# Value loads, the state update's bank and the second input product in the opening of a gated attention and feed-forward kernel

## The chip, the cores and the metric

The kernel runs on one core of a Trainium2 chip. The metric is the device time of one execution in microseconds (us). A second view is the profile of one execution, whose span runs from its first to its last instruction; all places in time ("at 63.95") are us from the start of that span.

## The reference

Two parts follow each other. The first is a gated linear attention: for each of 4 batches and 8 heads a state of 48 x 48 is carried over 768 tokens. The second is a feed-forward network over all 3072 tokens (4 x 768), with 384 inputs (8 heads x 48), 2048 hidden units and a leaky maximum.

```python
for t in range(S):
    state = alpha[:, :, t, :, None] * state + np.einsum('bhd,bhe->bhde', k[:, :, t], v[:, :, t])
    y[:, :, t] = np.einsum('bhd,bhde->bhe', q[:, :, t], state)
...
h = x @ w_in
g = np.maximum(0.01 * h, h)
return (g @ w_out).astype(np.float32)
```

q, k, v and alpha are float32. The two weights come as float64 and are read as pairs of 32-bit words.

## The kernel before, in words

**Units.** The attention is cut into 24 units: 6 blocks of 128 tokens, and in each block the 4 batches. Unit u is block u // 4 of batch u % 4. In a unit, the products of alpha along its 128 tokens turn the recurrence into matrix products: scores of keys against queries with a causal mask, times the values, plus the queries against the state that the earlier block of the same batch left. The first 9 units (0 to 8, AHEAD = 9) are done at the start, before the feed-forward part begins; units 9 to 23 are done later, mixed into it. Units 0 to 3 have no earlier state.

One of the first units goes through these functions:

- `load` (line 132) and `load_values` (156) issue transfers of alpha, q, k and v from SyncE's queue (SP). There are two buffers each for alpha, q and k and three for v, so a load of unit u + 2 (or u + 3 for v) takes the place of one that was used. From unit 9 on, the loads asked for early are put on a list and issued at the end of the weight loads.
- `turn_ahead` (295) transposes one of alpha, q, k on TensorE (PE) into a bank of PSUM, with `keep_warm` matmuls behind the first four, and then asks for the load that takes the buffer's place.
- `scans` (300) makes the running products on VectorE (DVE), and calls `next_state` for an earlier unit between its two scans.
- `scaled_q` (332), `scaled_k` (342), `scores` (352), `mask_scores` (361): scale, multiply on PE, copy to `sm` on ScalarE (ACT), mask on GpSimd (POOL). `mask_scores` then empties two lists on POOL: `scalings` (the new state, a product with the decay) and `parts` (see below).
- `outputs` (387) makes two PSUM banks of results y: the earlier state's part, then the masked scores times the values; then, in columns 256 to 447 of the first bank, the sum of keys times values `kv` for the state. For each of the two banks ACT makes a rounded copy in the high half of `large` (`xh`) and an exact copy `whole`; the difference, the low half, goes on the list `parts` for POOL (from unit 9 on DVE makes it at once).
- `next_state` (435) adds `kv` to the state on DVE (for units 0 to 3 ACT copies it), into `us`, and puts the scaling on the list.
- `gather` (449) moves, for three units, some rows of `large` to their places by two transfers. Gather 0, 1 and 2 belong to units 0 to 2, 3 to 5 and 6 to 8; each must wait until POOL has made the low halves of its units.

Where two engines read the same PSUM bank, the framework makes the second in the program's order wait for the first.

**Feed-forward.** The 16 blocks of 128 hidden units are the weight blocks. `load_weights` (199) fetches a block by four transfers of w_in and one of w_out into one of four buffers `raw`; `converting` (213) turns it into a high and a low float32 part in eight steps: ACT scales `raw`, DVE makes `bits` (two steps), `raw` and `pw`, ACT rounds the high half, DVE makes `raw` and the low half of `w`. Each step is put by hand between other work. An item is one weight block for the 384 tokens of three units. `ffn_in` (491) makes its input product (9 matmuls into `ph`), then ACT, DVE, ACT and DVE make `t`, `t`, `gh` and `gl`; conversion steps can be handed in to stand between these. `ffn_out` (518) makes its output product (9 matmuls), summed over all blocks in three PSUM banks, of tag b for the first three units and tag a for the next three. The first 32 items alternate between units 0 to 2 and units 3 to 5, block by block, while the blocks are converted. Output products follow their input products by two items, and by three from the ninth item on.

**What sets the order.** A helper at line 35 issues every operation behind the one before it on the same engine (so nearly all rows of the profile have line L35), until the third group of items begins. So in the opening each engine runs its instructions in the order in which they are written. The order of the opening is in lines 556 to 612: first loads, unit 0's start, a loop over units 0 to 7, then unit 8 (`last`), the conversion of block 1, and the first two items. In the loop, `WEIGHTS` says after which unit's scaling a weight block is asked for: block 1 at unit 5, block 2 at unit 6, block 3 at unit 7, each ahead of that unit's `outputs`; a gather stands behind the outputs. After the opening comes the main loop over items, whose first step asks for block 4; its transfers stand behind gather 2 in SP's queue.

Of the kernel before, what the change touches and what calls it, by code (L numbers as in the profile page):

```python
# [23 lines left out]
def gated_linear_attn_ffn(ctx, tc, q, k, v, alpha, w_in, w_out, out):  # L24
# [15 lines left out]
    B, H, S, D = q.shape  # L40
# [3 lines left out]
    C = 128  # L44
    NC = S // C
    NP = H // 2
# [4 lines left out]
    BR = HB + D  # L51
# [21 lines left out]
    AHEAD = 3 * UPB  # L73
# [8 lines left out]
    def bank(tag=None):  # L82
        if tag is None:
            tag = kinds[0]
            kinds.append(kinds.pop(0))
        return ps_x.tile([P, 512], F32, name=tag)
# [17 lines left out]
    state, vals_sb, rest = rest[:B], rest[B:B + NV], rest[B + NV:]  # L104
# [6 lines left out]
    def w_in_of(f, n, g):  # L111
        return w_sb[f][:, n, g * P:(g + 1) * P]
# [43 lines left out]
    def load_values(u):  # L156
        if u >= NU:
            return
        if u >= AHEAD and later is not None:
            later.append((load_values, u))  # L160
            return
        tb, b = units[u]
        made["v", u] = nc.sync.dma_start(
            vals_sb[u % NV].rearrange("t (h d) -> t h d", h=H),
            v[b, :, tb * C:(tb + 1) * C, :].rearrange("h t d -> t h d"),
        )
# [32 lines left out]
    def load_weights(f, part=None):  # L199

        if part != 1:
            jobs[f] = cvp.tile([P, 2 * NG, 2 * P], I32, name="raw", bufs=NRAW)
        raw = jobs[f]
        dst = raw.bitcast(I64) if f64 else raw[:, :, 0:P].bitcast(F32)
        for r, n, src, step, group in runs if part != 0 else ():
            a = w_in[src:src + n, f * P:(f + 1) * P]
            nc.sync.dma_start(
                dst[r:r + n, 0:NG], bass.AP(a.tensor, a.offset, [[step * DF, n], [group * DF, NG], list(a.ap[1])])
            )
        if part != 1:  # L210
            made["raw", f] = nc.sync.dma_start(dst[:, NG:], w_out[f * P:(f + 1) * P, :].rearrange("p (g f) -> p g f", g=NG))
# [71 lines left out]


    STEP = 16
    WEIGHTS = {5: 1, 6: 2, 7: 3}
    WARM = 16, 4, 3, 12
    warm = []

# [5 lines left out]
    def turn_ahead(u, i, name, **kw):  # L295
        turned[u, i] = transposed(u, i, name, **kw)
        if u < AHEAD:
            load(u + NL[i], i)
# [26 lines left out]
    def sum_up(u, which=(0, 1)):  # L325

        with behind("sm", u) if u >= AHEAD else nullcontext():
            for n in which:
                t = sums[u][n]
                nc.scalar.activation(t, t, AF.Abs, accum_out=acc[:, 2 * u + n:2 * u + n + 1])  # L330
# [11 lines left out]
    def scaled_k(u):  # L342
        pc, rc, pe, qs = live[u]
        turn_ahead(u, 2, "ks")
        kT = turned.pop((u, 2))
        if u >= AHEAD:
            load(u + NL[2], 2)
        ks = kT if u >= AHEAD else atp.tile([P, NP, C], F32, name="ks")
        made["ks", u] = nc.vector.tensor_tensor(ks, kT, rc, ALU.mult)
        live[u] = [pe, qs, ks]  # L350
# [36 lines left out]
    def outputs(u):  # L387
        tb, b = units[u]
        i, j = divmod(u, UPB)
        pe, qs, ktok = live[u][:3]  # L390
        V, W = vals_sb[u % NV], state[b]
        at = i % 3 * (NG + 1)
        banks = [bank(), bank()]
        y = [t.rearrange("r (p n) -> r p n", p=NP)[:, 0:2, :] for t in banks]

        def product(p, s, c, lhsT, rhs, **kw):

            nc.tensor.matmul(y[s][HB * c:HB * c + lhsT.shape[-1], p % 2, :], lhsT, rhs, skip_group_check=True, **kw)

        for n in range(2):  # L400
            for c in (0, 1):
                for s in (0, 1) if tb else ():
                    p, lo = 2 * c + n, HB * s
                    m = D if c else HB
                    product(p, s, c, W[lo:lo + D, p * D:p * D + m], qs[lo:lo + D, p, :], start=n == 0, stop=False)
        for n in range(2):
            for s in (0, 1):
                for c in (0, 1):
                    p = 2 * c + n
                    at_v, m = (2 * p + s) * D, D if c else HB  # L410
                    product(p, s, c, V[:, at_v:at_v + m], masked[u][s][:, p, :], start=not tb and n == 0, stop=n == 1)
        del masked[u]
        kv = None
        if tb < NC - 1:
            kv = banks[0][0:BR, 2 * C:2 * C + NP * D]
            for p in range(NP):
                for s, lo, m in ((0, 0, HB), (1, HB, D)):
                    h = 2 * p + s
                    made["kv", u] = nc.tensor.matmul(
                        kv[lo:lo + m, p * D:(p + 1) * D], ktok[:, p, lo:lo + m], V[:, h * D:(h + 1) * D],  # L420
                        start=True, stop=True, skip_group_check=True,
                    )
        load_values(u + NV)
        live[u] = pe, kv
        for s in (0, 1):
            xh, xl = (x_sb[0:BR, at + s:at + s + NG:2, n, j * C:(j + 1) * C] for n in (0, 1))
            nc.scalar.copy(xh, y[s][0:BR])
            if u < AHEAD:
                whole = atp.tile([P, 2, C], F32, name="whole")[0:BR]
                nc.scalar.copy(whole, y[s][0:BR])  # L430
                parts.append((xl, whole, xh.bitcast(F32), ALU.subtract))
            else:
                nc.vector.tensor_tensor(xl, y[s][0:BR], xh.bitcast(F32), ALU.subtract)

    def next_state(u):
        tb, b = units[u]
        pe, kv = live.pop(u)
        if kv is None:
            return
        W = state[b][0:BR]  # L440
        us = atp.tile([P, NP * D], F32, name="us")[0:BR]
        if tb == 0:
            nc.scalar.copy(us, kv)
        else:
            nc.vector.tensor_tensor(us, W, kv, ALU.add)
        W, us = (t.rearrange("d (p e) -> d p e", p=NP) for t in (W, us))
        scalings.append((W, us, pe[0:BR].broadcast_to([BR, NP, D]), ALU.mult))

    def gather(i):

# [40 lines left out]
    def ffn_in(i, f, steps=None):  # L491

        first, second = steps or ((), ())
        xh, xl = xs[i]
        ph = ps_h.tile([P, 512], F32, name="ph")[:, 0:TB]
        n = 0
        for g in range(NG):
            for wn, xt in ((HIGH, xh), (HIGH, xl), (LOW, xh)):
                nc.tensor.matmul(ph, w_in_of(f, wn, g), xt[:, g, :], start=n == 0, stop=n == 3 * NG - 1)
                n += 1  # L500
        t = ffp.tile([P, TB], F32, name="t")
        nc.scalar.mul(t, ph, 0.01)
        for step in first:
            next(step, None)
        nc.vector.tensor_tensor(t, ph, t, ALU.max)
        gh = ffp.tile([P, TB], F32R, name="gh", bufs=LAG + 1)
        nc.scalar.copy(gh, t)
        for step in second[:1]:
            next(step, None)
        gl = ffp.tile([P, TB], F32R, name="gl", bufs=LAG + 1)  # L510
        made["gl", i, f] = nc.vector.tensor_tensor(gl, t, gh.bitcast(F32), ALU.subtract)
        for step in second[1:]:
            next(step, None)
        return gh, gl
# [29 lines left out]
    items = []  # L544
# [3 lines left out]
    gs = {}  # L548
# [3 lines left out]
    def steps(conversion, n):  # L552
        for _ in range(n):
            next(conversion, None)
# [3 lines left out]
    load(0, 1)  # L558
    load(0, 2)
    load(1, 0)  # L560
    load_values(0)
    load(1, 1)
    load(1, 2)
    load_values(1)
    load_values(2)
    conversions = [converting(f) for f in range(EARLY + 2)]
    warm += WARM
    turn_ahead(0, 0, "e")
# [1 line left out]
    steps(conversions[0], 8)  # L570
    scaled_q(0)
    scaled_k(0)
    turn_ahead(1, 0, "e")
    for u in range(AHEAD - 1):
        scores(u)
        scans(u + 1, [u - 1] if u else [])
        mask_scores(u)
        k_tokens(u)
        scaled_q(u + 1)
        scaled_k(u + 1)  # L580
        if u + 2 < AHEAD:
            turn_ahead(u + 2, 0, "e")
        if u < AHEAD - 2:
            sum_up(u)
        else:
            steps(conversions[1], 1)
        if u in WEIGHTS:
            load_weights(WEIGHTS[u])
        outputs(u)
        if u % UPB == 0 and u:  # L590
            gather(u // UPB - 1)
            ready.add(u // UPB - 1)
    loaded_f = 1 + len(WEIGHTS)
    last = AHEAD - 1
    scores(last)
    mask_scores(last)
# [4 lines left out]
    gs[0] = ffn_in(*items[0][:2])  # L601
    new, coming = conversions[EARLY:]
    steps(new, 1)
    outputs(last)
    next_state(last)
    gs[1] = ffn_in(*items[1][:2], ((new, new), (new, new)))
    for todo in (scalings, parts):
        while todo:
            nc.gpsimd.tensor_tensor(*todo.pop(0))
# [5 lines left out]
    for n in range(len(items) + LAG):  # L615
# [3 lines left out]
        if n < len(items):  # L619
# [20 lines left out]
            elif i == 1:  # L640
                gs[n] = ffn_in(i, f, ((), (coming, coming, coming, coming)))
                new, coming = coming, converting(f + EARLY + 1)
# [148 lines left out]
```

## Time and profile before

| | us |
|---|---|
| median of 3 runs | 530.34 |
| lowest, highest | 529.16, 530.98 |
| profiled execution | 530.13 |
| its span | 528.4 |
| PE busy | 516.9 (98%) |
| DVE busy | 366.1 (69%) |
| ACT busy | 239.3 (45%) |
| POOL busy | 61.4 (12%) |

In rows of the timeline the columns are start, duration (from the first to the end of the last instruction merged in the row), engine, line, operation, tile written <- tiles read, sizes, and the count; in brackets the idle time of the engine before it and what ended that. SPq is the time in which SyncE issues a transfer, not the transfer itself. Tiles that stand in one allocation have one name: `small` holds the loads, the values and the states, `large` the inputs of the feed-forward part; a, b and ph are PSUM tags.

Rows of busy time by stretches have the length, then the busy time and count for each engine, the clock granted to PE (1.00 is full), the mean busy share of the DMA engines (transfers that overlap count twice, so it can pass 1) and GB/s.

### The profile page before, as it was taken

What the parts mean: (1) busy time and instruction counts of PE and PEld (TensorE: products, weight loads), DVE (VectorE), ACT (ScalarE), POOL (GpSimd) and SP (SyncE); (2) the same over time, 40 slices, a digit from 0 to 9 for tenths busy, and PEclk for the clock granted to TensorE, in tenths of its full rate; (3) what the DMA queues carried; (4) which work ended last, traced back from release to release, by engine and by line L of the source; (5) the groups of instructions that cost most, each with busy time, mean ns of one, the idle gap of its engine ahead of it and who ended that gap; (6) DMA issues with size and microseconds to landing.
All of it is one profiled execution on the core that took longest, in us unless ns stands there. A gap on an engine that the chain in (4) does not pass through costs nothing.

```text
span 528.4 us, 10355 instructions
## 1 busy us (share of the span) xinstructions
PE 516.9 (98%) x3986; PEld 495.0 (94%) x3986; DVE 366.1 (69%) x685; ACT 239.3 (45%) x533; POOL 61.4 (12%) x133
## 2 busy tenths in 40 slices
PE   8899899999999999999999999999999999999996
PEld 8788798999999899999999999999999999999996
DVE  6897799999969996787586585675787434333331
ACT  2597666656532544344334434345343444234332
POOL 2375810000000111000000000000000000000000
PEclk9999999999999999999999999999999999999999
DMA  9999885444905634442342422423301010101001
GB/s 155 166 162 158 188 176 167 130 133 140 203 3 143 174 91 98 94 102 70 71 107 42 115 69 58 93 56 87 70 1 39 1 46 2 24 0 47 0 1 50
DMA packets 92984, 46.65 MB, mean 88 GB/s; under 512 B 57857, under 2 KB 90113, under 8 KB 92929
## 3 DMA queue, kind: packets, MB, share of 16 engines
q1 hardware_dynamic: 92928, 45.93, 39.7%
q8 instruction: 33, 0.54, 0.4%
q14 instruction: 23, 0.18, 0.1%
HBM read 38.83 MB, written 4.72 MB: 82 GB/s over the span
## 4 chain that ended last, share of the span: by engine, by line
PE 85%; DVE 5%; DMA 4%; SPq 2%; ACT 1%; issue 1%; POOL 1%; DVEq 0%; ACTq 0%; POOLq 0%
PE ph L35 35%; PE b L35 34%; PE a L35 16%; SPq L35 2%; DMA small<-in_q_dram 1%; DMA small<-in_alpha_dram 1%; DVE t L35 1%; DVE gl L35 1%; DMA raw<-in_moe_w_out_dram 1%; POOL sm L35 1%; DVE bits L35 1%; DMA raw<-in_moe_w_in_dram 1%; DVE raw L35 1%; DVE pc L35 0%; ACT gh L35 0%
## 5 line engine op out<-in xcount | busy, mean ns | idle before, releaser
L35 PE MATMUL ph<-large,w 128*128 128x384 f32 x1152 | 223.4, 338 | 1.5 <-DVE w L35 1.0
L35 PEld LDWEIGHTS ph<-large,w 128*128 128x128 f32 x1152 | 200.6, 188 | 3.5 <-DVE w L35 1.4
L35 PE MATMUL b<-w,gh 128*128 128x384 f32 x672 | 173.8, 340 | 0.0
L35 DVE TENSOR_TENSOR t<-ph,t 128x384 f32<-128x384 f32 x128 | 70.4, 550 | 83.7 <-ACT t L35 83.7
L35 ACT ACTIVATE t<-ph 128x384 f32<-128x384 f32 x128 | 62.9, 492 | 139.5 <-PE ph L35 137.5
L35 PEld LDWEIGHTS b<-w,gh 128*128 128x128 f32 x672 | 119.9, 188 | 2.0 <-issue 0.5
L35 ACT CAST gh<-t 128x384 fp32r<-128x384 f32 x128 | 65.7, 514 | 106.4 <-DVE t L35 106.4
L35 PE MATMUL b<-w,gl 128*128 128x384 f32 x336 | 112.2, 335 | 0.0
L35 DVE TENSOR_TENSOR gl<-t,gh 128x384 fp32r<-128x384 f32 x128 | 70.9, 554 | 37.5 <-ACT gh L35 36.0
L35 PEld LDWEIGHTS b<-w,gl 128*128 128x128 f32 x336 | 63.0, 188 | 0.0
L35 POOL TENSOR_SCALAR_AFFINE_SELECT sm<-sm 128x512 f32<-128x512 f32 x33 | 23.5, 726 | 112.7 <-ACT sm L35 112.4
L35 PE MATMUL a<-qs,ks 48*128 48x128 f32 x312 | 29.8, 285 | 0.0
L35 PEld LDWEIGHTS a<-qs,ks 48*128 48x128 f32 x312 | 25.1, 187 | 4.3 <-issue 3.5
L35 DVE STREAM_TRANSPOSE ks<-small 128x512 f32<-128x512 f32 x15 | 16.7, 1123 | 14.6 <-PE a L35 14.0
L35 PE MATMUL a<-sm,small 128*48 128x128 f32 (+1 forms) x312 | 23.8, 279 | 0.9 <-POOL sm L35 0.9
L35 PE MATMUL a<-w,gh 128*128 128x384 f32 x96 | 24.6, 335 | 0.0
L35 POOL COPY pe<-pc 128x4 f32<-128x4 f32 x24 | 4.8, 200 | 165.9 <-DVE pc L35 165.9
L35 PEld LDWEIGHTS a<-sm,small 128*48 128x48 f32 (+1 forms) x312 | 16.9, 129 | 4.8 <-issue 3.1
L35 PE MATMUL ph<-small 128*128 128x128 f32 x120 | 16.9, 296 | 3.6 <-DMA small<-in_alpha_dram 2.0
L35 DVE TENSOR_TENSOR_SCAN pc<-e,small 128x128 f32<-128x128 f32 x60 | 20.0, 395 | 0.0
L35 DVE TENSOR_TENSOR_SCAN rc<-e,small 128x511 f32<-128x511 f32 x15 | 19.1, 1270 | 0.3
L35 POOL TENSOR_TENSOR small<-us,pe 112x192 f32<-112x192 f32 x20 | 10.5, 524 | 75.7 <-DVE us L35 69.3
(84 smaller groups left out, 545.2 us busy)
## 6 DMA issues: line engine op xcount, KB each, us to landing
raw<-in_moe_w_out_dram SPq DMA_DIRECT2D x16, 384.0 KB, 3.8
raw<-in_moe_w_in_dram SPq DMA_DIRECT2D x32, 144.0 KB, 3.2
small<-in_v_dram SPq DMA_DIRECT2D x24, 192.0 KB, 3.8
out_dram<-bits SPq DMA_DIRECT2D x18, 192.0 KB, 1.9
small<-in_alpha_dram SPq DMA_DIRECT2D x32, 96.0 KB, 2.3
small<-in_q_dram SPq DMA_DIRECT2D x30, 96.0 KB, 2.3
small<-in_k_dram SPq DMA_DIRECT2D x30, 96.0 KB, 2.2
small<-in_alpha_dram SPq DMA_DIRECT2D x30, 80.0 KB, 2.5
```

What stands on the lines that cost most here:

```text
L35: self.last = getattr(self.engine, op)(*args, **kw)
```

## The change

- The first three value loads are issued later: v0 behind unit 1's q and k, v1 behind unit 0's scaling (so behind unit 2's alpha, q and k), v2 in unit 0's pass behind unit 3's q and k.
- `kv` goes to the second y bank in place of the first. ACT's copies become a generator in two halves: the first bank's copies stay in `outputs`, and for units 0 to 7 the second bank's copies are made at the end of `next_state`, behind the sum that reads `kv`. Unit 8 makes both in `outputs`.
- Block 1 is still asked for at unit 5. Blocks 2 and 3 are asked for behind the outputs of units 6 and 7, so that block 2 comes behind gather 1.
- The second item's `ffn_in`, with four conversion steps of block 2 in it, stands ahead of unit 8's `outputs` and `next_state`.

```diff
-    WEIGHTS = {5: 1, 6: 2, 7: 3}
...
-            kv = banks[0][0:BR, 2 * C:2 * C + NP * D]
+            kv = banks[1][0:BR, 2 * C:2 * C + NP * D]
...
         load_values(u + NV)
         live[u] = pe, kv
+        rest = copies(u, at, j, y)
+        next(rest)
+        if u < AHEAD - 1:
+            halves[u] = rest
+        else:
+            next(rest, None)
+
+    def copies(u, at, j, y):
         for s in (0, 1):
             xh, xl = (x_sb[0:BR, at + s:at + s + NG:2, n, j * C:(j + 1) * C] for n in (0, 1))
             nc.scalar.copy(xh, y[s][0:BR])
...
                 nc.vector.tensor_tensor(xl, y[s][0:BR], xh.bitcast(F32), ALU.subtract)
+            yield
+
+    halves = {}
 
     def next_state(u):
...
         scalings.append((W, us, pe[0:BR].broadcast_to([BR, NP, D]), ALU.mult))
+        if u in halves:
+            next(halves.pop(u), None)
...
     load(1, 0)
-    load_values(0)
     load(1, 1)
     load(1, 2)
-    load_values(1)
-    load_values(2)
+    load_values(0)
...
     scaled_q(0)
     scaled_k(0)
+    load_values(1)
     turn_ahead(1, 0, "e")
...
         scaled_k(u + 1)
+        if not u:
+            load_values(2)
...
-        if u in WEIGHTS:
-            load_weights(WEIGHTS[u])
+        if u == AHEAD - 4:
+            load_weights(1)
         outputs(u)
         if u % UPB == 0 and u:
             gather(u // UPB - 1)
             ready.add(u // UPB - 1)
-    loaded_f = 1 + len(WEIGHTS)
+        if u > AHEAD - 4:
+            load_weights(u - AHEAD + 5)
+    loaded_f = 4
...
     steps(new, 1)
+    gs[1] = ffn_in(*items[1][:2], ((new, new), (new, new)))
     outputs(last)
     next_state(last)
-    gs[1] = ffn_in(*items[1][:2], ((new, new), (new, new)))
```

## The prediction before the result was known

> **What bounds the kernel now.** I read the page first, then busy time by stretches, then PE's row of the timeline from its idle times backwards.
>
> ```profile
> span 528.4 us, 10355 instructions
> PE 516.9 (98%) x3986; PEld 495.0 (94%) x3986; DVE 366.1 (69%) x685; ACT 239.3 (45%) x533; POOL 61.4 (12%) x133
> ```
> ```profile
> core 0: us, PE busy (x) PEld busy (x) DVE busy (x) ACT busy (x) POOL busy (x), PEclk, DMA share, GB/s
> 20.00:48.00 28.00, 27.98 (x413) 24.64 (x412) 24.32 (x55) 22.64 (x67) 18.05 (x39) 1.00 1.15 162
> 48.00:63.00 15.00, 12.62 (x205) 10.84 (x205) 11.57 (x22) 9.53 (x24) 10.63 (x15) 1.00 0.98 197
> 63.00:92.00 29.00, 27.96 (x165) 27.59 (x161) 27.41 (x45) 18.78 (x38) 4.23 (x5) 1.00 0.65 164
> 92.00:528.40 436.40, 431.83 (x3081) 416.26 (x3079) 288.83 (x534) 182.41 (x396) 23.66 (x56) 1.00 0.29 72
> ```
> From 92 us on PE is busy 431.83 of 436.40 us, so whatever comes early or late at 92 us comes so at the end. The change acts before that, and there are three limits in turn: transfers (DMA share 1.15) up to 48 us, the start of the feed-forward part, and DVE (27.41 of 29 us) from 63 to 92. PE's own rows show where each one ends last:
>
> ```profile
> 19.40 0.63 PE L35 MATMUL ph<-small 128*128 128x128 f32 x4 [1.68 <-DMA small<-in_alpha_dram]
> ...
> 48.38 0.66 PE L35 MATMUL ph<-small 128*128 128x128 f32 x4 [0.36 <-DMA small<-in_alpha_dram]
> ...
> 57.04 1.83 PE L35 MATMUL ph<-large,w 128*128 128x384 f32 x9
> ...
> 60.60 0.43 PE L35 MATMUL b<-sm,small 128*64 128x128 f32 x4 [1.15 <-POOL sm L35]
> 61.90 0.43 PE L35 MATMUL a<-sm,small 128*64 128x128 f32 x4 [0.87 <-POOL sm L35]
> ...
> 66.38 0.52 PE L35 MATMUL b<-w,gh 128*128 128x384 f32 x2
> ...
> 89.83 1.48 PE L35 MATMUL ph<-large,w 128*128 128x384 f32 x7 [1.04 <-DVE w L35]
> ```
> The last wait decides: at 89.83 PE has stood 1.04 us for the low half of weight block 5. So the end is set by the DVE chain that makes it, and PE time saved before 89.83 only lengthens this wait. Followed back, the DVE chain begins where ACT gets weight block 1 (55.40, a transfer):
>
> ```profile
> 55.40 0.92 ACT L35 ACTIVATE raw<-raw 128x768 f32<-128x768 f32 x1 [1.66 <-DMA raw<-in_moe_w_out_dram]
> ...
> 62.27 0.95 ACT L35 ACTIVATE raw<-raw 128x768 f32<-128x768 f32 x1
> 63.27 0.37 ACT L35 CAST large<-b 112x256 fp32r<-112x256 f32 x1
> ...
> 75.61 0.93 ACT L35 ACTIVATE raw<-raw 128x768 f32<-128x768 f32 x1
> 76.42 0.49 ACT L35 ACTIVATE t<-ph 128x384 f32<-128x384 f32 x1
> ```
> ```profile
> 62.40 0.57 DVE L35 TENSOR_TENSOR gl<-t,gh 128x384 fp32r<-128x384 f32 x1 [0.58 <-ACT gh L35]
> 63.95 0.35 DVE L35 TENSOR_TENSOR us<-small,b 112x192 f32<-112x192 f32 x1 [0.99 <-ACT whole L35]
> 64.23 0.56 DVE L35 TENSOR_SCALAR bits<-raw 128x768 int32<-128x768 int32 x1
> 64.83 1.14 DVE L35 SCALAR_TENSOR_TENSOR bits<-raw,bits 128x768 int32<-128x768 int32 x1
> ...
> 67.93 0.55 DVE L35 TENSOR_SCALAR pw<-bits 128x768 int32<-128x768 int32 x1
> 68.40 0.55 DVE L35 TENSOR_TENSOR t<-ph,t 128x384 f32<-128x384 f32 x1
> ...
> 77.27 0.55 DVE L35 TENSOR_TENSOR t<-ph,t 128x384 f32<-128x384 f32 x1
> ...
> 88.83 0.95 DVE L35 SCALAR_TENSOR_TENSOR w<-raw,pw 128x768 fp32r<-128x768 f32 x1
> ```
> After 63.95 no DVE row of this stretch carries a wait of note: what delays one of its steps delays block 5.
>
> **Value loads moved back.** Alpha of unit 2 now stands behind both v1 and v2:
>
> ```profile
> 11.37 2.18 SPq L35 DMA_DIRECT2D small<-in_v_dram  x2
> 13.66 2.32 SPq L35 DMA_DIRECT2D small<-in_alpha_dram  x1
> ```
> It moves up by those two issues, about 2.2 us, more than PE's wait of 1.68 at 19.40: that wait goes. The values cost nothing: v0, v1, v2 stay in SP's queue ahead of the alpha of units 2, 3, 4, whose transposes stand in PE's queue ahead of the outputs that read them. What is late next is alpha of unit 8. From alpha of unit 4 on the queue is as before, with the same bytes ahead; the transfers run without a pause (share 1.15, 162 GB/s), and PE already waits 0.36 us at 48.38. An earlier PE waits there for 0.36 + 1.68 = 2.04 us instead. Weight block 1, which ACT waits 1.66 us for at 55.40, is behind the same bytes too. I take nothing for this edit; its other end is -1.68 us (a rival below).
>
> **State update in the second bank, second copies behind it.** No instruction is added. For units 4 to 7 DVE's us step no longer waits for ACT's copies of the bank that holds the sum; ACT's second pair of copies waits for us instead. Units 4 to 6 lie before 48.38 or just around it, where PE waits for the transfer anyway: nothing. At the end, unit 7's second pair goes behind unit 8's score copies, so POOL's masking may start up to 0.7 us sooner (two ACT copies of 0.37, as at 63.27). That only shortens the PE waits at 60.60 and 61.90. Unit 8 itself does both pairs first, so its us keeps its wait for ACT.
>
> **Second input product ahead of unit 8's outputs.** On PE nine matmuls, at most 1.83 us as at 57.04, fill the waits of 1.15 and 0.87 us at 60.60 and 61.90. Its input, gather 1, is issued ahead of weight block 2, so about where that block starts now:
>
> ```profile
> 53.06 2.43 SPq L35 DMA_DIRECT2D raw<-in_moe_w_in_dram  x4
> ...
> 56.23 1.22 SPq L35 DMA_DIRECT2D large<-large  x2
> ```
> It comes 3.17 us sooner; block 2 comes later by the gather's 1.22 us of issue. PE gains up to 1.83 us, but loses it at the next step: the first output product (66.38) needs three banks of tag b, one of them unit 8's first y bank. ACT's copies free it, and ACT now does block 2's scaling, t and gh of the second product ahead of these copies. DVE's steps (bits twice, t, below) end about 2.1 us after 63.25, gh takes some 0.5 as t does on ACT (0.49 at 76.42), the two copies at most 0.74: the bank is free at about 66.5. PE stands where it stood at 66.38: nothing. If the bank were free at once, PE would be earlier and would wait longer for DVE at 89.83; nothing too.
>
> On DVE the 0.99 us wait at 63.95 goes, because block 2's conversion no longer stands behind us. ACT has scaled block 2 at 62.27 + 0.95 = 63.22 if the block lands in time, so bits starts at 63.25 instead of 64.23. With us (0.28 to the next row) behind, the chain gains about 0.7 us.
>
> **What the move does to POOL and SP.** us of unit 8 now stands behind bits, t, raw, gl and pw. In the rows these take from 64.23 to 68.40, 4.17 us, some 0.7 of which comes from sharing with POOL (bits 1.14 where others take 0.95, and a longer gl). So us starts at 63.25 + 3.5 to 4.2 = 66.75 to 67.4 and is done at 67.1 to 67.7, where now it is done at 64.3. POOL's last list waits for it:
>
> ```profile
> 54.55 1.42 POOL L35 TENSOR_TENSOR large<-whole,large 112x256 fp32r<-112x256 f32 x2
> 58.01 3.83 POOL L35 TENSOR_SCALAR_AFFINE_SELECT sm<-sm 128x512 f32<-128x512 f32 x2 [2.04 <-ACT sm L35]
> 61.82 1.74 POOL L35 TENSOR_TENSOR large<-whole,large 112x256 fp32r<-112x256 f32 x2
> 63.52 0.51 POOL L35 TENSOR_TENSOR small<-us,pe 112x192 f32<-112x192 f32 x1
> 64.39 0.77 POOL L35 TENSOR_TENSOR small<-us,pe 112x192 f32<-112x192 f32 x1 [0.36 <-DVE us L35]
> 65.12 2.47 POOL L35 TENSOR_TENSOR large<-whole,large 112x256 fp32r<-112x256 f32 x2
> ```
> Now: state of 8 at 64.39, two subtractions, done at 67.59. After the change three subtractions follow the state, since unit 7's second one is listed only after unit 8's masking. One costs 0.71 us alone (54.55), 0.87 at 61.82, 1.24 beside a busy DVE (65.12). POOL's end: at least 67.1 + 0.51 + 3 x 0.71 = 69.75, at most 67.7 + 0.77 + 3 x 1.24 = 72.2. DVE is as busy there as at 65.12, but its t steps and the us read one operand from PSUM, so I take 1.05 each: 67.3 + 0.6 + 3.15 = 71.0.
>
> The SBUF page of the Trainium skill (SBUF — State Buffer, Who interferes with whom) states that a DVE instruction with two SBUF inputs and a GpSimd one that reads SBUF exclude each other, and that the second to issue is blocked until the first is done. The trace agrees in kind (3.83 us for two selects at 58.01 beside DVE's conversion, 2.47 against 1.42 us for the subtractions); by that rule alone the sum would go to the upper end, 72.2.
>
> Behind POOL's end stand, in SP's queue, gather 2 and then weight block 4:
>
> ```profile
> 67.62 1.21 SPq L35 DMA_DIRECT2D large<-large  x2
> ...
> 71.34 0.58 SPq L35 DMA_DIRECT2D raw<-in_moe_w_out_dram  x1
> ```
> ```profile
> raw<-in_moe_w_out_dram SPq DMA_DIRECT2D x1, 384.0 KB, 3.9
> ```
> The last row is the answer on transfers for that one issue: 3.9 us to landing. So block 4 lands 71.34 - 67.62 + 3.9 = 7.6 us after POOL's end, now at 75.2. ACT scales it at 75.61: 0.4 us in hand. Behind the scaling in ACT's order stands t (76.42, done at 76.91), which DVE takes at 77.27: another 0.36. Nothing else can run in that place, since ACT and DVE take their steps in the written order. Together 0.7 to 0.8 us are in hand, and POOL's end moves by 71.0 - 67.6 = 3.4. DVE's t at 77.27 is then late by 3.4 - 0.7 = **2.7 us** (bounds: 69.75 gives 1.4, 72.2 gives 3.9). The 0.7 us that DVE gained before is swallowed in the wait. From 77.27 to 89.78 DVE has no gap to win it back in; PE, which waits for DVE at 89.83, starts as much later, and after 92 us it is full to the end.
>
> **The sum.** 0 (loads) + 0 (bank) + 0 (PE's product) + 2.7 (block 4): the profiled execution took 530.13 us (528.4 of span and 1.7 around it), 0.2 below the median of 530.34. So 530.13 + 2.7 = 532.8, likeliest 531.5 to 534.0.
>
> **Rivals.** (1) Block 4 is not late: POOL ends before about 68.3. For it: nothing but how rough spans on POOL are. Against: us alone comes 2.8 us later. Then only DVE's 0.7 us counts: 529.4. (2) The transfers do move up with PE, because SP's queue is held by PE's reading of the buffers and not by the transfers: the 1.68 us reach weight block 1 at 55.40 and all that follows. For it: many SP issues take 1 us or more and PE reads buffers just before. Against: share 1.15, and the wait at 48.38 falls on a transfer. With block 4 late all the same: 530.13 + 2.7 - 1.68 = 531.2. (3) Both, the faster side: 530.13 - 1.68 - 0.7 = 527.8; it needs alpha of unit 8 landing by 46.7 and POOL's end not over 0.7 us behind the shifted DVE. (4) The change does not fill PE's wait, since gather 1 lands too late for the second product: PE then waits at the product instead, and the chain over block 4 is as in the forecast, so its time is too.
>
> **Chances.** Forecast with (4): 0.62; (1) 0.13; (2) 0.15; (3) 0.08; 0.02 for anything else. A measurement here tells about 0.3%, 1.6 us, from no change. Slower by more: nearly all of the forecast, 0.60. Within: (1), (2), the forecast's low edge, 0.31. Faster: 0.09. The range reaches down to (1), 529.4, and up to 534.0.
>
> **What would show it.** Right: no alpha wait near 18 us and one of about 2 us before unit 8's transposes at 48.4; nine more ph matmuls ahead of the sm waits, which shrink; bits at 63.3; DVE's last us on the small state near 67; POOL's last large at 70 to 72; gather 2 right behind it; an ACT wait of 2 to 4 us on raw from w_out near 78; PE's wait for w at 89.8 grown to about 3 us in all. Wrong: unit 8's alpha or weight block 1 more than 1 us earlier; gather 2 issued before 68.3; no ACT wait on block 4; or PE resuming block 5 before 90 us.

## The result and the profile after

The kernel after takes 535.25 us (median of 5 runs, 534.96 to 537.24), the kernel before 530.41 beside it (529.16 to 531.06): a ratio of 1.0104, 95% interval 1.0078 to 1.0130. It is slower: the two medians differ by 4.84 us, and the ratio makes 5.5 us of 530.41. The profiled execution took 535.13 us, with a span of 533.4.

The first two lines of the page of after show PE's busy time up by 3.7 us and the span by 5.0:

```profile
span 533.4 us, 10346 instructions
PE 520.6 (98%) x3986; PEld 497.0 (93%) x3986; DVE 368.6 (69%) x685; ACT 240.3 (45%) x533; POOL 60.3 (11%) x133
```
Busy time by the stretches of the prediction, kernel after:

```profile
48.00:63.00 15.00, 15.00 (x219) 13.20 (x219) 11.44 (x20) 8.35 (x20) 8.34 (x13) 1.00 0.97 204
63.00:92.00 29.00, 24.43 (x124) 22.40 (x123) 24.61 (x40) 15.74 (x33) 4.40 (x4) 0.94 0.56 146
92.00:528.40 436.40, 435.67 (x3099) 419.92 (x3098) 292.95 (x540) 184.07 (x401) 23.57 (x56) 1.00 0.28 71
```
PE is now busy in the whole of 48 to 63, where it had stood 2.38 us, and loses more than that from 63 to 92: 24.43 of 29 us, where it had 27.96. DVE falls there from 27.41 to 24.61. That the engine which bounds this stretch has idle time again says that something ahead of it is late.

Four rows of the timeline of after, one each of POOL, SP's queue, ACT and DVE, are the chain of the prediction in order:

```profile
67.70 0.51 POOL L35 TENSOR_TENSOR small<-us,pe 112x192 f32<-112x192 f32 x1 [6.85 <-DVE us L35]
68.16 3.93 POOL L35 TENSOR_TENSOR large<-whole,large 112x256 fp32r<-112x256 f32 x3
```
```profile
72.12 1.21 SPq L35 DMA_DIRECT2D large<-large  x2
73.44 2.37 SPq L35 DMA_DIRECT2D raw<-in_moe_w_in_dram  x4
75.86 0.58 SPq L35 DMA_DIRECT2D raw<-in_moe_w_out_dram  x1
```
```profile
79.87 0.90 ACT L35 ACTIVATE raw<-raw 128x768 f32<-128x768 f32 x1 [3.69 <-DMA raw<-in_moe_w_out_dram]
```
```profile
81.18 0.56 DVE L35 TENSOR_TENSOR t<-ph,t 128x384 f32<-128x384 f32 x1 [3.34 <-ACT t L35]
```
POOL waits 6.85 us for us of unit 8 and ends at 72.09 (before: 67.59). Gather 2 stands right behind it (72.12), weight block 4 behind that (75.86, before 71.34), ACT waits 3.69 us for block 4, and DVE's t of the sixth item starts at 81.18, 3.91 us later than before. PE's rows with a wait, from 63 us on:

```profile
65.65 0.62 PE L35 MATMUL b<-w,gh 128*128 128x384 f32 x2 [0.62 <-DVE t L35]
66.74 1.83 PE L35 MATMUL ph<-large,w 128*128 128x384 f32 x9 [0.30 <-ACT whole L35]
71.56 1.48 PE L35 MATMUL ph<-large,w 128*128 128x384 f32 x7 [1.08 <-DVE w L35]
81.79 1.83 PE L35 MATMUL ph<-large,w 128*128 128x384 f32 x9 [0.81 <-DVE t L35]
...
87.54 2.31 PE L35 MATMUL ph<-large,w 128*128 128x384 f32 x7 [1.52 <-DVE w L35]
100.62 1.50 PE L35 MATMUL ph<-large,w 128*128 128x384 f32 x7 [0.29 <-DVE w L35]
```
With the 0.23 us at 85.43, which is left out here, these waits sum to 4.85 us, more than the nine matmuls that PE won at 57; before, only the 1.04 us at 89.83 stood here. Compared product by product, the input products start 4.5 to 4.6 us later than before from 102 to 168 us, 5.3 later from 192 to 426 and 5.0 later at the end.

**The zero of a single profile.** ACT starts to scale weight block 1 at 55.40 in the profile of before and at 54.72 in that of after. In the profiles of the experiments below it starts between 54.51 and 56.27; with the old order of the loads alone the four profiles have 54.79, 54.97, 55.40 and 56.27. These are single executions of different kernels, but before and delay_block4 differ in nothing ahead of this row, and they are 0.61 us apart. The nine profiles with the new loads have 54.51 to 55.09, so a part of the 0.68 us may also be a gain of the loads; one execution each can't tell. The end varies as well: from the t of the last item to the end of the span seven profiles take 9.6 to 9.8 us and six take 11.2 to 12.5, so only the spans of before and after, with 9.8 us each, are set side by side here. All later times of the opening are therefore counted from ACT's start on block 1: block 4's w_out issue and DVE's t of the sixth item, each minus ACT's start on block 1 in the same profile. For before these are 71.34 - 55.40 = 15.94 and 77.27 - 55.40 = 21.87; the table has the difference to these.

| kernel | ratio (95%) | ACT starts block 1 | block 4 issued later by | DVE's t later by |
|---|---|---|---|---|
| after | 1.0104 (1.0078-1.0130) | 54.72 | 5.20 | 4.59 |
| loads_alone | 0.9993 (0.9975-1.0011) | 54.68 | 0.01 | 0.01 |
| bank_alone | 1.0030 (1.0016-1.0044) | 54.97 | 2.28 | 1.82 |
| product_alone | 1.0053 (1.0034-1.0071) | 56.27 | 3.04 | 2.40 |
| after_without_bank | 1.0031 (1.0015-1.0046) | 54.52 | 3.02 | 2.39 |
| product_back | 1.0040 (1.0024-1.0056) | 54.77 | 2.35 | 2.53 |
| drain_early | 1.0061 (1.0043-1.0080) | 54.51 | 3.95 | 3.33 |
| delay_block4 | 1.0049 (1.0029-1.0069) | 54.79 | 2.60 | 1.75 |
| block4_first | 1.0016 (1.0000-1.0032) | 55.09 | early | 1.14 |
| no_bank_block4_first | 0.9993 (0.9977-1.0010) | 54.85 | early | 0.77 |
| drain_block4_first | 1.0012 (0.9995-1.0029) | 55.06 | early | 1.12 |
| dve_waits_filled | 0.9996 (0.9981-1.0012) | 54.70 | early | 0.35 |

In after, product_alone, after_without_bank and drain_early, where ACT waits 1.85 to 3.69 us for block 4, DVE's t is late by block 4's delay less 0.61 to 0.64 us. In delay_block4 it is less 0.85; there ACT has the block 3.78 us behind its issue (77.11 - 73.33), in these four 3.97 to 4.01. In bank_alone and product_back block 4 is later too, but t is not late because of it: ACT starts on the block 0.15 and 0.08 us behind its step before. Where these two lose is said below.

### The profile page after: what moved, and what is told of

It is laid out like the page before. It is cut to its first block, busy times and chain, and to the rows that moved or that the text cites. A ratio compares the mean times of both kernels' runs of the same rounds, so it can differ in the third digit from the quotient of the medians.

```text
span 533.4 us, 10346 instructions
## 1 busy us (share of the span) xinstructions
PE 520.6 (98%) x3986; PEld 497.0 (93%) x3986; DVE 368.6 (69%) x685; ACT 240.3 (45%) x533; POOL 60.3 (11%) x133
## 3 DMA queue, kind: packets, MB, share of 16 engines
HBM read 38.83 MB, written 4.72 MB: 82 GB/s over the span
## 4 chain that ended last, share of the span: by engine, by line
PE 78%; DVE 3%; ACT 1%; issue 0%; DMA 0%; DVEq 0%; SPq 0%; ACTq 0%
PE ph L35 34%; PE b L35 32%; PE a L35 13%; DVE t L35 1%; DVE gl L35 0%; DVE pc L35 0%; DVE raw L35 0%; DMA small<-in_q_dram 0%; DVE e L35 0%; DVE w L35 0%; DVE rc L35 0%; DVE ks L35 0%; ACT gh L35 0%; ACT t L35 0%; ACT bits L35 0%
## 5 line engine op out<-in xcount | busy, mean ns | idle before, releaser
L35 POOL TENSOR_SCALAR_AFFINE_SELECT sm<-sm 128x512 f32<-128x512 f32 x33 | 21.5, 664 | 115.1 <-ACT sm L35 115.0
L35 PEld LDWEIGHTS a<-sm,small 128*64 128x64 f32 (+1 forms) x312 | 17.1, 129 | 3.5 <-issue 2.9
L35 ACT ACTIVATE raw<-raw 128x768 f32<-128x768 f32 x16 | 14.7, 921 | 11.0 <-DMA raw<-in_moe_w_out_dram 11.0
```

What stands on the lines that cost most here:

```text
L35: self.last = getattr(self.engine, op)(*args, **kw)
```

## The experiments

**Block 4 ahead of gather 2, in the kernel after** (block4_first). The expectation speaks of blocks 4 and 5; the kernel that ran moves block 4 alone.

```diff
+    load_weights(4)
+    loaded_f = 5
     gather(2)
     ready.add(2)
```


> The changed kernel with weight blocks 4 and 5 asked for ahead of gather 2. Theory (block 4 is late behind POOL's last list): ACT's wait of 3.69 us on block 4's transfer is gone, DVE's t of item 5 comes at about 77.8 instead of 81.18, block 5's low half is done at about 90.3 instead of 93.7, and the time is 530 to 531 (before 530.4, changed 535.3). Rival (PE's idle times and half clock around the early product are the cost, block 4's wait only fills slack): the ACT wait goes, the time stays at 533 or more.

Measured: 532.64 us, ratio 1.0016 (1.0000 to 1.0032). POOL's end is as late as in after (68.51 + 3.93 = 72.44), but block 4 is issued at 63.78 and ACT's row has no wait left:

```profile
76.44 0.92 ACT L35 ACTIVATE raw<-raw 128x768 f32<-128x768 f32 x1
```
So 0.9 of the 1.04 per cent hang on block 4 standing behind POOL's last list. The expected 77.8 for t came as 78.10, and the expected 530 to 531 us were missed: 1.14 us of t's delay are left. The late list itself, with gather 2 behind it, costs little where no weight block waits for it.

**The delay alone, in the kernel before** (delay_block4). Six transfers of 24 KB into an unused tile are put between gather 2 and block 4; all else is as before.

```diff
     gather(2)
+    scrap = cst.tile([P, 6, D], F32, name="scrap")
+    for n in range(6):
+        nc.sync.dma_start(scrap[:, n, :], q[0, n, 0:P, :])
     ready.add(2)
```


> The kernel before with six added small transfers (24 KB each, read by nobody) in SP's queue between gather 2 and weight block 4: some 0.5 us of issue each, so block 4 lands near 78.3 instead of 75.2, and nothing else is touched. Theory (block 4 has 0.7 us in hand and then delays DVE one for one): ACT waits about 2.5 us for block 4, DVE's t of item 5 comes at 79.6 to 79.8, the time is 2.3 to 2.6 us longer. Rival (PE's order and clock make the loss): ACT waits, but the end moves by under 1 us.

Measured: 533.64 us, 1.0049 (1.0029 to 1.0069). SP's queue, and then the same rows of ACT and DVE:

```profile
66.71 1.21 SPq L35 DMA_DIRECT2D large<-large  x2
68.02 2.94 SPq L35 DMA_DIRECT2D scrap<-in_q_dram  x6
71.05 2.24 SPq L35 DMA_DIRECT2D raw<-in_moe_w_in_dram  x4
73.33 0.58 SPq L35 DMA_DIRECT2D raw<-in_moe_w_out_dram  x1
```
```profile
77.11 0.90 ACT L35 ACTIVATE raw<-raw 128x768 f32<-128x768 f32 x1 [1.84 <-DMA raw<-in_moe_w_out_dram]
```
```profile
78.41 0.56 DVE L35 TENSOR_TENSOR t<-ph,t 128x384 f32<-128x384 f32 x1 [1.49 <-ACT t L35]
```
A later block 4 alone, with nothing else of the change, makes the kernel before slower through the same three rows. ACT's wait fell short of the expected 2.5 us, and t is 1.75 us late; the time is 2.6 us longer, and its interval, 1.5 to 3.7 us, holds both. So for the whole change the path over block 4 is shown from both sides.

**The loads alone, in the kernel before** (loads_alone).

```diff
     load(1, 0)
-    load_values(0)
     load(1, 1)
     load(1, 2)
-    load_values(1)
-    load_values(2)
+    load_values(0)
...
     scaled_k(0)
+    load_values(1)
...
         scaled_k(u + 1)
+        if not u:
+            load_values(2)
```


> The kernel before with the new order of the first value loads alone. Theory (the transfers set the pace up to 48 us): PE's wait near 18 us goes, a wait of about 2 us stands before unit 8's alpha, block 1 lands within 0.7 us of 55.3: 529.4 to 530.6. Rival (the transfers move up with PE): block 1 lands 1.7 us earlier, 528.7.

Measured: 531.11 us, 0.9993 (0.9975 to 1.0011): nothing that can be told from no change, and a chain from block 1 on that is the same to 0.01 us. The interval leaves room for a gain of up to 0.25 per cent, 1.3 us.

**The second product and the order of gather 1 and block 2 alone, in the kernel before** (product_alone).

```diff
-    WEIGHTS = {5: 1, 6: 2, 7: 3}
...
-        if u in WEIGHTS:
-            load_weights(WEIGHTS[u])
+        if u == AHEAD - 4:
+            load_weights(1)
...
+        if u > AHEAD - 4:
+            load_weights(u - AHEAD + 5)
+    loaded_f = 4
...
     steps(new, 1)
+    gs[1] = ffn_in(*items[1][:2], ((new, new), (new, new)))
     outputs(last)
     next_state(last)
-    gs[1] = ffn_in(*items[1][:2], ((new, new), (new, new)))
```


> The kernel before with the second input product ahead of unit 8's outputs, and gather 1 ahead of block 2, alone; loads and bank as before. Theory: unit 8's state step comes near 67.3 and two subtractions instead of three follow it on POOL, which ends near 70.8 and puts block 4 at 78.4, 2.4 to 3.3 us too late for ACT: 533 to 533.8, less than the whole change by the one subtraction that the half copies add (1.2 us). Rival (the third subtraction does not count): 535.

Measured: 534.53 us, 1.0053 (1.0034 to 1.0071). POOL waits 4.01 us for us, makes two subtractions (69.33, 2.16 us) and ends at 71.49 in an execution whose block 1 came 0.87 us later than in before. DVE's t is 2.40 us late. The move of the product alone starts the chain.

**The product put back, in the kernel after** (product_back): loads, bank and order of transfers stay, the second product stands behind unit 8's state again.

```diff
-    gs[1] = ffn_in(*items[1][:2], ((new, new), (new, new)))
     outputs(last)
     next_state(last)
+    gs[1] = ffn_in(*items[1][:2], ((new, new), (new, new)))
```


> The changed kernel with the second input product behind unit 8's outputs and state step again; loads, bank and gather order as changed. Theory: the state step of unit 8 comes near 64 again, POOL ends near 69 with three subtractions, block 4 lands near 76.7, at most 0.7 us too late: 530 to 531.3. Rival (loads or bank carry part of the loss): 532 or more.

Measured: 533.70 us, 1.0040 (1.0024 to 1.0056), more than the forecast's working left for the other edits together. Block 4 is not what makes t late here:

```profile
77.02 0.92 ACT L35 ACTIVATE raw<-raw 128x768 f32<-128x768 f32 x1
78.65 0.49 ACT L35 ACTIVATE t<-ph 128x384 f32<-128x384 f32 x1 [0.71 <-PE ph L35]
```
ACT scales block 4 at once and then waits for PE, which ran at half clock from 72.98 to 76.39 in this profile (last section); DVE's t at 79.17 waits 0.58 us for this step. The rest of its 2.53 us is close to the 1.82 us of the next run, the bank edit alone.

**The bank edit alone, in the kernel before** (bank_alone).

```diff
-            kv = banks[0][0:BR, 2 * C:2 * C + NP * D]
+            kv = banks[1][0:BR, 2 * C:2 * C + NP * D]
...
+        rest = copies(u, at, j, y)
+        next(rest)
+        if u < AHEAD - 1:
+            halves[u] = rest
+        else:
+            next(rest, None)
...
+        if u in halves:
+            next(halves.pop(u), None)
```


> The kernel before with the state update in the second bank and the half copies alone. Theory: unit 8's state step now waits for both pairs of copies (about 0.5 us more in DVE's chain), and three subtractions behind it end POOL near 69.5, so block 4 lands 1.9 us later, 1 us too late: 0.8 to 1.5 us slower. Rival (the earlier state steps of units 4 to 7 gain): 0.5 us faster.

Measured: 532.57 us, 1.0030 (1.0016 to 1.0044). POOL's rows in this kernel, from unit 8's masking on:

```profile
57.17 1.70 POOL L35 TENSOR_SCALAR_AFFINE_SELECT sm<-sm 128x512 f32<-128x512 f32 x2 [1.54 <-ACT sm L35]
58.84 1.03 POOL L35 TENSOR_TENSOR large<-whole,large 112x256 fp32r<-112x256 f32 x1
59.83 1.22 POOL L35 TENSOR_TENSOR small<-us,pe 112x192 f32<-112x192 f32 x1
65.23 0.77 POOL L35 TENSOR_TENSOR small<-us,pe 112x192 f32<-112x192 f32 x1 [4.17 <-DVE us L35]
65.96 3.48 POOL L35 TENSOR_TENSOR large<-whole,large 112x256 fp32r<-112x256 f32 x3
```
Three things are dearer than in before. The two selects take 1.70 us where they took 3.83, so POOL's work of unit 7 now falls into DVE's conversion of block 1. One more subtraction stands in the last list. And unit 8's us waits 1.33 us for ACT's copies (before 0.99), since kv is now in the bank that is copied second.

The expectation had this loss come over block 4. It comes on DVE itself:

```profile
77.23 0.93 ACT L35 ACTIVATE raw<-raw 128x768 f32<-128x768 f32 x1
```
```profile
77.79 0.95 DVE L35 SCALAR_TENSOR_TENSOR w<-raw,pw 128x768 fp32r<-128x768 f32 x1
78.66 0.55 DVE L35 TENSOR_TENSOR t<-ph,t 128x384 f32<-128x384 f32 x1
```
ACT has block 4 nearly in time and DVE's t follows w without a wait. Yet t is 1.82 us late: us of unit 8 starts 9.83 us behind ACT's start on block 1 instead of 8.55, and from us to t it is 13.86 us instead of 13.32, where pw takes 1.10 us beside POOL's subtractions in place of 0.55.

**The bank edit undone, in the kernel after** (after_without_bank): kv in the first bank and all four copies in outputs, the rest of the change kept.

```diff
-            kv = banks[1][0:BR, 2 * C:2 * C + NP * D]
+            kv = banks[0][0:BR, 2 * C:2 * C + NP * D]
...
-        rest = copies(u, at, j, y)
-        next(rest)
-        if u < AHEAD - 1:
-            halves[u] = rest
-        else:
-            next(rest, None)
-
-    def copies(u, at, j, y):
...
-            yield
-
-    halves = {}
...
-        if u in halves:
-            next(halves.pop(u), None)
```


> The kernel after with the bank edit undone: kv stands in the first y bank again and all four copies of a unit stand in outputs. Loads, second product and transfers stay as in the kernel after. Theory (the late block 4 costs most, the bank edit adds a third subtraction to POOL's last list and a longer wait for unit 8's us): POOL's list has two subtractions and ends near 70.8 (71.49 with the old loads, less 0.7), gather 2 right behind; the first matmuls of the input products are 2.6 us later than before from 100 us on (3.27 with the old loads, less 0.7), ratio 1.004 to 1.0055. Rival (the bank edit costs nothing inside this change, and the excess over the forecast comes from the half clock near 88): input products 4.0 to 4.6 us later as in the kernel after, ratio about 1.009.

Measured: 533.38 us, 1.0031 (1.0015 to 1.0046), with POOL's end at 69.72 and the input products 1.51 us later by the clock. That is less than the theory had, and far from the rival's 1.009: within the change the bank edit costs at least as much as the rest. POOL's last rows, and the conversion of block 1 on DVE in this kernel and then in after:

```profile
57.13 3.78 POOL L35 TENSOR_SCALAR_AFFINE_SELECT sm<-sm 128x512 f32<-128x512 f32 x2 [1.71 <-ACT sm L35]
60.88 1.74 POOL L35 TENSOR_TENSOR large<-whole,large 112x256 fp32r<-112x256 f32 x2
62.59 0.50 POOL L35 TENSOR_TENSOR small<-us,pe 112x192 f32<-112x192 f32 x1
67.10 0.51 POOL L35 TENSOR_TENSOR small<-us,pe 112x192 f32<-112x192 f32 x1 [4.00 <-DVE us L35]
67.56 2.16 POOL L35 TENSOR_TENSOR large<-whole,large 112x256 fp32r<-112x256 f32 x2
```
```profile
57.21 0.55 DVE L35 TENSOR_SCALAR raw<-raw 128x768 int32<-128x768 int32 x1
57.68 0.55 DVE L35 TENSOR_SCALAR pw<-bits 128x768 int32<-128x768 int32 x1
58.15 0.95 DVE L35 SCALAR_TENSOR_TENSOR raw<-raw 128x768 f32<-128x768 uint32 x1
59.13 1.29 DVE L35 SCALAR_TENSOR_TENSOR w<-raw,pw 128x768 fp32r<-128x768 f32 x1
```
```profile
57.41 0.73 DVE L35 TENSOR_SCALAR raw<-raw 128x768 int32<-128x768 int32 x1
58.05 0.98 DVE L35 TENSOR_SCALAR pw<-bits 128x768 int32<-128x768 int32 x1
58.96 1.59 DVE L35 SCALAR_TENSOR_TENSOR raw<-raw 128x768 f32<-128x768 uint32 x1
60.58 1.08 DVE L35 SCALAR_TENSOR_TENSOR w<-raw,pw 128x768 fp32r<-128x768 f32 x1
```
Without the bank edit POOL's selects are the ones that are held (3.78 us) and DVE's steps are short; with it, DVE's three steps before w take 0.73, 0.98 and 1.59 us and w starts 5.86 us behind ACT's start on block 1, not 4.61. The other kernels without the bank edit, dve_waits_filled with its other order left aside, have 4.61 to 4.72 us there too, and the six with it 5.75 to 5.99.

**POOL's lists emptied once more, in the kernel after** (drain_early), behind unit 7's state step, so that one subtraction moves out of the last list.

```diff
     next_state(last - 1)
+    for todo in (scalings, parts):
+        while todo:
+            nc.gpsimd.tensor_tensor(*todo.pop(0))
```


> The changed kernel with POOL's lists emptied once more behind unit 7's state step, so that unit 7's second subtraction doesn't stand behind unit 8's state. Theory (each subtraction there is worth 1.2 to 1.3 us of block 4's delay): POOL ends near 70.8, ACT's wait is some 1.3 us shorter than the 3.69 of the changed kernel, the time is 1.0 to 1.3 us under the changed kernel's, so 1.0065 to 1.008 of the kernel before. Rival (the third subtraction hides): no difference, 1.010.

Measured: 533.99 us, 1.0061 (1.0043 to 1.0080). The last list has two subtractions of 2.51 us and ends at 70.64, 1.45 us sooner than in after; t is late by 3.33 us in place of 4.59. Moving the third subtraction is worth 1.26 us.

**Both remedies with block 4 first.** no_bank_block4_first is after_without_bank with block 4 ahead of gather 2; drain_block4_first is drain_early with block 4 ahead of gather 2. The edits are those above.

> The kernel after with the bank edit undone and weight block 4 asked for ahead of gather 2. Theory (with block 4 in time only the DVE chain's own length counts, and the bank edit lengthened it): ACT gets block 4 without a wait, the input products come 0.3 us earlier to 0.4 later than before, ratio 0.998 to 1.001. Rival (what was left in the run with block 4 first comes from the second product's place, not from the bank): 0.8 us later as there, ratio 1.0015 to 1.002.

> The kernel after with POOL's lists emptied once more behind unit 7's state step and weight block 4 asked for ahead of gather 2. Theory (what was left with block 4 first, 0.84 us at 100 us, is DVE held up by POOL's three subtractions beside it at 68.5 to 72.4): one subtraction fewer there leaves 0.4 to 0.6 us, ratio 1.0005 to 1.001. Rival (it is left by the chain of unit 8's copies and PE's waits, whatever POOL does): 0.8 us still, ratio 1.0016.

Measured: 531.05 us, 0.9993 (0.9977 to 1.0010), and 532.39 us, 1.0012 (0.9995 to 1.0029). With block 4 in time and the bank edit undone the input products are 0.23 us later by the clock (t is 0.77 us late counted from block 1), and nothing of the loss is left that can be measured in the time. The drain with block 4 first is like block4_first (t late by 1.12 and 1.14 us): what is left there is not the third subtraction beside DVE at 68 to 72. The expected 0.4 to 0.6 us did not come.

**A version meant to be faster** (dve_waits_filled): the kernel before with the new loads, block 4 ahead of gather 2, and two conversion steps moved into DVE's waits at 62.40 and 63.95.

```diff
...
-    steps(conversions[1], 5)
-    gs[0] = ffn_in(*items[0][:2])
+    steps(conversions[1], 4)
+    gs[0] = ffn_in(*items[0][:2], ((), (conversions[1],)))
...
     outputs(last)
+    steps(new, 1)
     next_state(last)
-    gs[1] = ffn_in(*items[1][:2], ((new, new), (new, new)))
+    gs[1] = ffn_in(*items[1][:2], ((new,), (new, new)))
...
+    load_weights(4)
+    loaded_f = 5
     gather(2)
```


> The kernel before with the new order of the value loads, block 4 ahead of gather 2, and two steps of DVE put in its waits: block 1's last step between t and gl of the first item, block 2's first bits step ahead of unit 8's state step. Theory (DVE's chain sets the end up to block 5, PE has 1.04 us of wait there): the waits of 0.58 and 0.99 us go, 1.0 us or a little less is gained, and up to 0.7 from the loads: 0.9965 to 0.998 of the kernel before. Rival (PE sets it): no difference, 0.9985 to 1.0.

Measured: 530.91 us, 0.9996 (0.9981 to 1.0012). The step of block 1 filled the first wait, but the step put into the second did not run in it. DVE's rows, then POOL's:

```profile
60.62 1.01 DVE L35 TENSOR_TENSOR gl<-t,gh 128x384 fp32r<-128x384 f32 x1
63.40 0.56 DVE L35 TENSOR_SCALAR bits<-raw 128x768 int32<-128x768 int32 x1 [1.77 <-POOL small L35]
```
```profile
61.19 1.71 POOL L35 TENSOR_TENSOR large<-whole,large 112x256 fp32r<-112x256 f32 x2
62.86 0.50 POOL L35 TENSOR_TENSOR small<-us,pe 112x192 f32<-112x192 f32 x1
```
bits starts 0.04 us after POOL's state step of unit 7 ends (62.86 + 0.50), and this is a wait of the program: among the semaphores that bits waits for in the trace is one that POOL alone raises. It carries this wait in before and in after too. It reads no tile that POOL writes there; why the framework puts the wait in is not shown. No version here beats the kernel before.

## Why the prediction was right or wrong, point by point

The direction and the path were right, the size was not: +5.0 us in the profiled execution where 2.7 was forecast, with the top of the range at 3.9.

**Where the 2.7 us fell short.** They were 3.4 us of POOL's end less 0.7 us in hand. Counted from ACT's start on block 1, t is 4.59 us late. Of the 1.9 us between, 1.0 is the start of bits, which stands 8.85 us behind ACT's start on block 1 and not at the forecast's 63.25 - 55.40 = 7.85. The three subtractions are 0.8, at 3.93 us and not 3.15, and 0.1 is the time in hand, 0.61 us and not 0.7. So the step that failed is bits at 63.25. It took the work ahead of bits to be as long as before, but the bank edit, put at nothing, makes block 1's conversion 1.0 us longer; and where that work is as before, bits waits for POOL (both below). The price of a subtraction was also too low. By the clock t is 3.91 us late, since block 1 came 0.68 us sooner in this execution, and 0.67 and 0.42 us more arise behind t: 5.0 in all.

**Loads: 0. Right, as far as the noise allows.** PE's 1.68 us at 19.40 is gone. It comes back, though not in one piece: over four stretches from 14 to 49 us PE is busy 32.93 of 35 us before and 33.10 after, as the sums of the two views show.

```profile
sum 35.00, PE 32.93 PEld 28.80 DVE 30.23 ACT 26.38 POOL 20.59; mean PE 8.23 PEld 7.20 DVE 7.56 ACT 6.59 POOL 5.15
```
```profile
sum 35.00, PE 33.10 PEld 29.07 DVE 30.99 ACT 27.65 POOL 21.73; mean PE 8.28 PEld 7.27 DVE 7.75 ACT 6.91 POOL 5.43
```
After, PE waits 0.78 us for an alpha at 36.54, 0.49 for k at 46.77 and 0.46 for alpha of unit 8 at 47.86; the forecast had put the whole 2 us at that last place. The stretch is bound by transfers, as said. Rival 2 (transfers move up with PE) would have made loads_alone 1.68 us faster, 0.32 per cent; its interval ends at 0.25.

**Bank: 0. Wrong.** The step "That only shortens the PE waits at 60.60 and 61.90" looked at who waits for POOL's masking and not at what POOL and DVE do to each other when it starts sooner. Alone the edit costs 0.30 per cent; on top of the rest it takes the ratio from 1.0031 to 1.0104 and t from 2.39 to 4.59 us late. Of these 2.20 us, 1.26 are the third subtraction (drain_early). The other 0.94 are us of unit 8, which starts 0.57 us later for its chain (12.72 us behind ACT's start on block 1 in drain_early, 12.15 in after_without_bank), and the two subtractions left, 2.51 us in place of 2.16. The third subtraction did stand in the forecast, in POOL's list at 1.05 us. What it had at nothing is the longer conversion of block 1. Without the bank edit t is 2.39 us late, under the forecast.

**Second product: nothing for PE, 0.7 us for DVE. Half right.** PE's nine matmuls fill the waits, and it stands again at the outputs (0.62 and 0.30 us at 65.65 and 66.74). But DVE gained nothing: bits starts at 63.57, not 63.25, 8.85 us behind ACT's start on block 1 where before had 64.23 - 55.40 = 8.83. Block 1's conversion, which ends 1.0 us later under the bank edit (61.66 - 54.72 against 61.36 - 55.40), used the gain up: t and gh of the first item come later by this, and ACT's scaling of block 2 behind them. Without the bank edit there is no such stretch, and bits still waits for POOL, here in after_without_bank:

```profile
63.12 0.56 DVE L35 TENSOR_SCALAR bits<-raw 128x768 int32<-128x768 int32 x1 [1.09 <-POOL small L35]
```
That is 63.12 - 54.52 = 8.60, a gain of 0.23. The working had only the wait of us for ACT in view. In before POOL's state step of unit 7 runs to 63.52 + 0.51 = 64.03, so bits, which waits for it, could not have started at 63.25.

**POOL's last list: end at 71.0, bounds 69.75 to 72.2. Mis-sized.** The clock time of us was right (67.27; 66.75 to 67.4 forecast), but only because block 1 came 0.68 us sooner in this execution; behind ACT's start on block 1 it came 4.00 us later than in before, not the 2.8 to 3.45 of the working. One subtraction took 3.93 / 3 = 1.31 us, above the 1.24 of the upper bound, and not 1.05. The reason given for 1.05, that DVE's t steps read one operand from PSUM, did not hold: the three subtractions ran from 68.16 to 72.09, and of this time DVE's t steps fill 0.6 us; raw, gl and w fill the most of it, and gl and w are long there (1.10 and 1.48 us, elsewhere 0.55 and 0.95).

The rows thus bear out the upper end: POOL ends at 72.09 by the clock, and counted from ACT's start on block 1 it ends 5.18 us later than in before, which from 67.59 makes 72.77, past the bound. The Trainium skill (SBUF — State Buffer, Who interferes with whom) says that whichever of DVE and GpSimd issues first holds the shared ports and blocks the other fully; by that rule alone the prediction named 72.2, and the measured end by the clock is 72.09.

**Block 4 and the 0.7 us in hand. Right.** Gather 2 is issued 0.03 us behind POOL's end, block 4 3.74 us behind gather 2 (before 3.72), and t's delay is block 4's less 0.61 us.

**Behind t: as late at the end as at 77.27. Short by about 1 us.** In three of the profiles PE is late at the end of the first items by just what t is: 1.51 and 1.51 in after_without_bank, 3.27 and 3.27 in product_alone, 2.44 and 2.53 in drain_early, all against before and by the clock. In after it is 3.91 and 4.58. There PE's granted clock falls to half from 87.91 to 91.32:

```profile
84.50:87.91 3.41, 1.66 (x8) 1.05 (x8) 3.41 (x7) 1.83 (x4) 0.00 (x0) 1.00 0.85 251
87.91:91.32 3.41, 3.41 (x13) 3.41 (x12) 3.26 (x7) 2.36 (x5) 0.00 (x0) 0.50 0.67 224
```
The seven matmuls at 87.54 take 2.31 us where seven take 1.48, the next t is late, and PE waits once more for w at 100.62. That explains the 0.67 us of this profile. Two other executions of after have spans of 533.3 and 533.5 us at a mean clock of 0.999 and 1.000, so without a half-clock stretch like this one; what made those two as long stays open. The last 0.4 us arise from 173 us on, where the order is not written by hand: from the 37th input product PE does other work first, there and in block4_first, but not in drain_block4_first. Why the order comes out so was not tried.

**Rivals.** (1) block 4 not late: refuted by ACT's 3.69 us. (3) fell with (1) and (2). (4) gather 1 too late for the product: no, PE is busy in the whole of 48 to 63.

## What to carry to other kernels

A list that an engine off the critical path empties late costs little by itself; ask which transfers stand behind it in the queue, because putting one weight block ahead of the gather took back 0.9 of 1.04 per cent here. Before a wait is counted as a gain, look up every semaphore (the counter by which one engine waits for another) of the step that is to fill it: bits waited for POOL as well as for ACT. When an edit lets POOL start sooner, look up which DVE steps it now lands beside, and cost both engines at the slow end of the rows they share. Before two profiles are compared by the clock, set both to one early event that the change does not touch: here the start on block 1 came 0.7 us sooner after the change, by chance or by the loads, and hid part of the loss.

## What the runs showed of the hardware

**POOL and DVE hold each other up in both directions.** Two selects took 3.78 us beside a DVE conversion that kept its short steps, and 1.68 us when they started 0.4 us sooner, counted from ACT's start on block 1, and DVE's steps grew instead. Over all profiles the seven kernels without the bank edit have selects of 3.77 to 3.90 us that start 2.60 to 2.62 us behind ACT's start; the six with it have 1.54 to 1.84 us and start at 2.06 to 2.54. A subtraction on POOL takes 0.71 us alone (54.55 in before) and 1.31 in after's last list, beside which DVE's gl and w grow to 1.10 and 1.48 us.

**Half clock came behind half-idle stretches, but not behind all of them.** Before the 3.41 us at half clock PE had been busy 1.66 of 3.41 us in after. In product_back it was the same: busy 1.82 of 3.41 us from 69.57 to 72.98, then 3.41 us at 0.50. In after the stretch before, with 2.71 of 3.41 us busy, was followed by full clock. But so were 1.79 us in drain_early (68.46 to 71.87) and 1.81 in drain_block4_first (69.85 to 73.26), less than the 1.82 of product_back. So the busy share alone does not decide it, and what does stays open.

The Trainium skill (TensorE: Matmul & The Clock Gate, Part 1: The HAM clock gate) gives the same window of 3413 ns, but speaks of an idle window; here the windows ahead of half clock were busy for about half.
